# 64x32 in place of 64x64 tiles on TensorE for both layers of a convolution and GELU network

## The chip, the cores and the metric

The kernel runs on one core of a Trainium2 chip. The metric is device time in microseconds (us), the time of the one core. TensorE (PE in the profile) multiplies; a weight load (PEld) puts the stationary operand into its array and a matmul streams the moving operand through it. ScalarE is ACT, VectorE is DVE, GpSimd is POOL, and SP's queue issues most DMAs.

## What is computed

A causal depthwise convolution with 7 taps over 8 sequences of 4096 tokens and 192 channels, with softmax weights that each group of 24 channels shares, and behind it two dense layers with an exact GELU between them.

```python
def _attn_ref(x, weight):                      # x 8 x 4096 x 192, weight 8 x 7
    w = softmax(weight, axis=-1)
    x_pad = concatenate([zeros((B, 6, D)), x], axis=1)
    idx = arange(S)[:, None] + arange(7)[None, :]
    x_unf = x_pad[:, idx, :].reshape(B, S, 7, 8, 24)
    return einsum('hk,bskhg->bshg', w, x_unf).reshape(B, S, D)

def _moe_ref(x, w_in, w_out):                  # 32768 x 192, 192 x 2048, 2048 x 192
    h = x @ w_in
    g = 0.5 * h * (1.0 + erf(h / sqrt(2)))
    return g @ w_out
```

## The kernel before

**Blocks.** The 32768 tokens are cut into two halves of 16384 that are worked on together: the lower 64 partitions hold one half, the upper 64 the other, each with 64 of the 192 channels, in three passes (NP = 3). The tokens of a half come in blocks: six of 256 (n = 0 to 5), then 29 of 512 (n = 6 to 34; M0 is 6, M1 is 34).

**One block.** SP loads the tokens, VectorE transposes them (L516) and runs the convolution tap by tap (L537, L544), the last tap writing `xc` in bf16. In the first two blocks TensorE does the convolution instead (`pconv`, L708), with diagonal weights. Then the first layer: `mm1(n, i)` (L729) makes one slice of `hp`, 128 of the 2048 hidden units by 512 tokens of both halves. ScalarE applies GELU from `hp` to `gT` (L674), one slice at a time; `hp` has two buffers. The second layer multiplies `gT` by `wout` into `ob`.

**Tiles of TensorE.** A matmul names a tile of the 128x128 array by `tile_position=(row, column)`. The moving operand's 64 partitions choose the row half (0 or 64), the output's partitions choose the column strip. Matmuls on different tiles can run side by side.

First layer, L766: for each slice three passes p, in each both row halves `hf`, and within these `fw` output rows at a time (`fo`). In the 256-token blocks and block 6, `fw` is 128 (one 64x128 tile for each row half; 64 in two slices of block 0); in blocks 7 to 34, `M0 < n <= M1`, it is 64: four 64x64 tiles in the order (0,0), (0,64), (64,0), (64,64), twelve matmuls a slice, each over 512 tokens. Each row half has its own PSUM bank (offset `o`).

Second layer, L837, in `mm2_t(m, ps, i)` (L821) for blocks 6 to 33: three passes `ps`, in each 16 steps `i`, and in a step two row halves `hf` by two token halves `h`: four 64x64 tiles in the same order, each over 512 tokens. Here `wout` is stationary, `gT` moves, and the output is 64 channels by 512 tokens in a bank of `ob`; `h` chooses output partitions 0 to 63 or 64 to 127. VectorE transposes the finished bank into `osb` (L343), and SP stores it. Blocks 0 to 5 use an older form (`mm2`, L806), and the last block a 128x128 form (L889).

**Order on TensorE.** It is written out by hand. While block n's first layer runs, the second layer of block n - 1 is dealt out between its slices: after slice i come `SHARE[i]` of its 48 units, `(ps, i)`. Waits on semaphores stand at the head of a slice (GELU has emptied the buffer two slices back, L735; the convolution is done, L740 and L757) and at the head of a pass of the second layer (L826, L828, L831). The last matmul of a slice adds to `S_MM1`, which lets GELU start; the last one of a pass adds to `S_PH` or `S_MM2`, which lets VectorE empty the bank.

Of the kernel before, what the change touches and what calls it, by code (L numbers as in the profile page):

```python
# [11 lines left out]
def bass_lightweight_conv__then__act_gelu_exact_kernel(  # L12
# [10 lines left out]
    F2, C = moe_w_out.shape  # L23
# [18 lines left out]
    NP = D // 64  # L42
    NF = F // 128
# [29 lines left out]
    M0, M1 = 6, NB - 1  # L73
# [13 lines left out]
    CH = [[2 * CG[hf][i // 2] + i % 2 for i in range(NF)] for hf in range(2)]  # L87
# [9 lines left out]
    def sbt(name, shape, dt):  # L97
        return es.enter_context(nc.sbuf_tensor(name, shape, dt))
# [7 lines left out]
    def ap(t, off, pat):  # L106
        return bass.AP(t, off, pat)

    with es:
        win = sbt("win", [128, NP * F], BF16)  # L110
        wout = sbt("wout", [128, NF * C], BF16)
# [16 lines left out]
        gT = [sbt("gT%d" % i, [128, NF * 2 * TB], BF16) for i in range(2)]  # L128
# [38 lines left out]
        def bank(b, r=slice(0, 128), w=512):  # L167
            return ob[r, 512 * (b % 4) : 512 * (b % 4) + w]
# [4 lines left out]
        def hbuf(u, r=slice(0, 128), o=0, w=2 * TB):  # L173

            if u < SL0[1] and u % 3 == 2:
                return ob[r, 2 * TB + o : 2 * TB + o + w]
            return hp[u % 3 if u < SL0[1] else u % 2][r, o : o + w]
# [36 lines left out]
        def wait_pc(e, n, p):  # L214

            if n == 0:
                e.wait_ge(S_PCA, p + 1)
                if p >= 1:
                    e.wait_ge(S_PCE, p)
            else:  # L220
                e.wait_ge(S_PCA, len(PA) + 1)
                if p >= 1:
                    e.wait_ge(S_PCE, len(PV) + (0, 2, 5)[p])
# [31 lines left out]
        def cvd(n):  # L255

            return sum(NCV - 2 * (m in K0) for m in range(n + 1) if m not in PC)
# [6 lines left out]
        def banks(m, g):  # L264


            if m < M0:
                return [bank(2 * ((G0[m] + g) % 2) + h, w=C) for h in range(2)]
            if g % 2:
                return [hp[g // 2][:, h * TB : h * TB + C] for h in range(2)]  # L270
            r = NP * (M1 - 1 - M0)
            return [bank(b, w=C) for b in sorted((b % 4 for b in ((r + 3, r), (r + 1, r + 2))[g // 2]))]
# [60 lines left out]
        def ring(m, j):  # L333
            return NP * (m - M0) + j
# [350 lines left out]
        def _(t):  # L685
# [43 lines left out]
            def mm1(n, i):  # L729
                w, c = WS[n], NCH[n]  # L730
                u = SL0[n] + i
                if n == 0 and u >= 3:
                    t.wait_ge(S_GELU, u - 2)
                elif u >= SL0[1]:
                    t.wait_ge(S_GELU, u - 1)  # L735
                if i == 0:
                    if n in PC:
                        wait_pc(t, n, NP - 2)
                    else:
                        t.wait_ge(S_CV, cvd(n) - 1)  # L740
                if n == 0:
                    for j in {0: (0, 1), 2: (2, 5), 4: (3,), 6: (4,)}.get(i, ()):
                        t.wait_ge(S_WIN[j], 16)
                    if i in (1, 3, 4, 6):
                        t.wait_ge(S_DUPE, (0, 1, 0, 3, 4, 0, 5)[i])
                        if i == 1:
                            t.wait_ge(S_DUPP, 1)
                todo = [(cc, p) for cc in range(c) for p in range(NP)]
                head = (n, i) == (0, 0)
                if head:  # L750
                    todo.sort(key=lambda q: q[1] == NP - 1)
                for cc, p in todo:
                    if i == 0 and cc == 0 and p == NP - 1:
                        if n in PC:
                            wait_pc(t, n, p)
                        else:
                            t.wait_ge(S_CV, cvd(n))  # L757
                    for hf in range(2):
                        r = slice(64 * hf, 64 * hf + 64)
                        ch = CH[hf][i * c + cc]  # L760
                        f0 = FQ * ((ch // 2) ^ hf) + ch % 2
                        fw = 64 if (n == 0 and 4 <= i <= 5) or M0 < n <= M1 else 128
                        for fo in range(0, 128, fw):
                            f1 = 64 * hf * NP * F + p * F + f0 + 2 * fo
                            o = hf * TB + cc * w
                            ins = t.matmul(  # L766
                                hbuf(u, slice(fo, fo + fw), o, w),
                                ap(win, f1, [[NP * F, 64], [2, fw]]),
                                xc[n % 2][r, p * TB : p * TB + w],
                                start=(p == 0 and (cc == 0 or not head)),  # L770
                                stop=(p == NP - 1 and (cc == c - 1 or not head)),
                                tile_position=(64 * hf, fo),
                            )
                ins.then_inc(S_MM1)
# [46 lines left out]
            def mm2_t(m, ps, i):  # L821

                w = WS[m]
                if i == 0:
                    if ps < 2:
                        t.wait_ge(S_EV, EVC[m] - (1 if m == M0 else 2) + ps)  # L826
                    if ps > 0:
                        t.wait_ge(S_PH, PHC[m] + ps)  # L828
                if ps == 0 and i % 4 == 0:

                    t.wait_ge(S_GELU, SL0[m] + i + 4)  # L831
                for hf in range(2):
                    j = UPLO[ps][hf]
                    r = slice(64 * hf, 64 * hf + 64)
                    for h in range(2):
                        c0 = (2 * i + h) * w
                        ins = t.matmul(  # L837
                            bank(ring(m, j), slice(64 * h, 64 * h + 64), w),
                            ap(
                                wout,  # L840
                                64 * hf * NF * C + CH[h][i] * C + j,
                                [[NF * C, 64], [NP, 64]],
                            ),
                            gT[m % 2][r, c0 : c0 + w],
                            start=(i == 0 and (ps == 0 or (ps, hf) == (1, 1))),
                            stop=(i == NF - 1 and (ps == 2 or (ps, hf) == (1, 0))),
                            tile_position=(64 * hf, 64 * h),
                        )
                if i == NF - 1:
                    ins.then_inc(S_MM2 if ps == 2 else S_PH)  # L850

# [12 lines left out]
            for n in range(NB):  # L864
                todo = units(max(n - 1, 0))
                if n < 2:
                    todo = [(g, ph, k) for ph, k0, k1 in ORD0 for g in range(2) for k in range(k0, k1)]
                    todo = todo[12:] if n else todo[:12]
                for i in range(NSL[n]):
                    mm1(n, i)  # L870
                    for q in behind.get((n, i), []):
                        pconv(*q)
                    new = M0 < n <= M1
                    ws = SHARE if new else [0] * 7 + [1] if n == 0 else [1] * NSL[n]
                    a0 = len(todo) * sum(ws[:i]) // sum(ws)
                    a1 = len(todo) * sum(ws[: i + 1]) // sum(ws)
                    for un in todo[a0:a1]:
                        if n < 2 and un[:2] == (0, int(un[2] // 4 == 1)) and un[2] % 4 == 0:
                            t.wait_ge(S_WOUT[un[2] // 4], 16)
                        (mm2_t if new else mm2)(max(n - 1, 0), *un)  # L880
            m = NB - 1
            for g in range(NG[m]):
                wait_banks(t, m, g)
                for h in range(2):
                    for i in range(NF):
                        if (g, h) == (0, 0) and i % 4 == 0:
                            t.wait_ge(S_GELU, SL0[m] + i + 4)
                        c0 = (2 * i * NG[m] + 2 * g + h) * 128
                        ins = t.matmul(  # L889
                            banks(m, g)[h],  # L890
                            gT[m % 2][:, c0 : c0 + 128],
                            wout[:, CH[h][i] * C : (CH[h][i] + 1) * C],
                            start=(i == 0),
                            stop=(i == NF - 1),
                        )
# [47 lines left out]
```

## Time and profile before

| what | value |
|---|---|
| two runs, median | 678.76 us (678.42 and 679.11) |
| the profiled execution's span | 676.8 us |
| granted TensorE clock in the span | 1.000 |
| matmuls and weight loads | 12504 of each |
| L766 on 64x64 tiles, 512 tokens | 5376 matmuls, 376 ns each; 64x64 loads 107 ns |
| L837 on 64x64 tiles, 512 tokens | 5376 matmuls, 376 ns each; 64x64 loads 118 ns |
| first and last start of these matmuls | 83.37 and 663.35 us |
| GELU of one slice (L674) | 1023 ns |

The span reaches from the program's first to its last instruction in one profiled execution; the runs' time also holds what lies around it. In a row of the groups the columns are the line, the engine, the operation, output and inputs with their shapes, and the count; behind the bar the busy time and the mean time of one, and behind the next bar the engine's idle time before them and what ended it. Ends of matmuls are modelled, so that several matmuls overlap in the trace: the distance of their starts tells the pace, not their length.

### The profile page before, as it was taken

To read this page: it belongs to the slowest core of one execution; us is meant where nothing else is said; L and a number is where in the kernel's file an instruction comes from. 1 tells how busy PE (TensorE), PEld (TensorE's weight loads), DVE (VectorE), ACT (ScalarE), POOL (GpSimd) and SP (SyncE) were. 2 spreads that over 40 slices of the span, in tenths; PEclk is the share of its full clock that TensorE was granted. 3 is DMA by queue.
4 is the path that set the end of the run, shared out by engine and by line. 5 is a ranking of instruction groups with operands and counts; after the bars stand their busy time and mean duration, and the time that the engine had idled before them with its cause. 6 is when DMAs were issued, how large, how long until landed. Compare 5 with 4: busy or idle time off the path is not lost.

```text
span 676.8 us, 26873 instructions
## 1 busy us (share of the span) xinstructions
PE 673.1 (99%) x12504; PEld 413.7 (61%) x12504; DVE 526.4 (78%) x607; ACT 536.5 (79%) x551; POOL 35.7 (5%) x61
## 2 busy tenths in 40 slices
PE   9999999999999999999999999999999999999998
PEld 8999555555555555555555555555555555555557
DVE  6989977987778977779777788777797777887511
ACT  8998977887778777777877787877877777778773
POOL 7010000000000000000000000000000000000000
PEclk9999999999999999999999999999999999999999
DMA  9435324223444224442234431244422344310223
GB/s 155 117 93 122 72 60 96 71 46 76 96 95 92 50 52 96 95 96 67 43 84 96 95 91 44 57 96 95 96 58 51 84 96 95 83 42 22 49 48 95
DMA packets 133280, 53.64 MB, mean 79 GB/s; under 512 B 126384, under 2 KB 133104, under 8 KB 133168
## 3 DMA queue, kind: packets, MB, share of 16 engines
q1 hardware_dynamic: 129136, 49.37, 32.6%
q0 software_dynamic: 2912, 1.97, 2.0%
q8 instruction: 98, 1.61, 1.0%
q10 hardware_dynamic: 1120, 0.59, 0.3%
q14 instruction: 14, 0.11, 0.1%
HBM read 28.31 MB, written 25.17 MB: 79 GB/s over the span
## 4 chain that ended last, share of the span: by engine, by line
PE 98%; ACT 1%; DVE 0%; DMA 0%; issue 0%; ACTq 0%
PE hp L766 49%; PE ob L837 43%; PE ob L806 5%; PE ob L889 1%; PE hp L889 1%; ACT gT L674 1%; DMA wsb<-in_weight_dram 0%; ACT xc L210 0%; PE ob L708 0%; ACT dg L621 0%; DVE wcol L488 0%; ACT osb L314 0%; ACT wex L608 0%; ACT xTb L238 0%; DVE wnm L479 0%
## 5 line engine op out<-in xcount | busy, mean ns | idle before, releaser
L674 ACT ACTIVATE gT<-hp 128x1024 bf16<-128x1024 f32 x510 | 520.9, 1023 | 127.6 <-PE hp L766 123.9
L766 PE MATMUL hp<-xc,win 64*64 64x512 bf16 (+2 forms) x6036 | 417.3, 366 | 0.3
L837 PE MATMUL ob<-gT,wout 64*64 64x512 bf16 x5376 | 366.4, 376 | 0.0
L544 DVE SCALAR_TENSOR_TENSOR acc<-xT,wcol,acc 128x1024 f32<-128x1024 f32 (+1 forms) x330 | 295.4, 945 | 3.5 <-ACT acc L645 3.5
L766 PEld LDWEIGHTS hp<-xc,win 64*64 64x64 bf16 (+1 forms) x6036 | 189.3, 106 | 131.4 <-issue 0.3
L837 PEld LDWEIGHTS ob<-gT,wout 64*64 64x64 bf16 x5376 | 172.3, 118 | 122.8
L343 DVE STREAM_TRANSPOSE osb<-ob 128x512 f32<-128x512 f32 x84 | 74.4, 888 | 129.1 <-PE ob L837 129.1
L516 DVE STREAM_TRANSPOSE xT<-xin 128x1536 f32<-128x1536 f32 (+2 forms) x39 | 74.8, 1925 | 2.0 <-DMA xin<-in_x_dram 2.0
L544 DVE SCALAR_TENSOR_TENSOR xc<-xT,wcol,acc 128x1024 bf16<-128x1024 f32 (+1 forms) x66 | 60.6, 958 | 0.0
L443 POOL COPY xT<-xT 128x18 f32<-128x18 f32 x30 | 22.6, 753 | 510.3 <-DVE xT L516 487.0
L806 PE MATMUL ob<-wout,gT 64*128 64x192 bf16 x768 | 41.6, 243 | 0.0
L806 PEld LDWEIGHTS ob<-wout,gT 64*128 64x128 bf16 x768 | 34.2, 94 | 4.2
L537 DVE TENSOR_SCALAR acc<-xT,wcol 128x512 f32<-128x512 f32 (+2 forms) x60 | 33.7, 604 | 1.1
L688 PE MATMUL hp<-const-bfloat16-1.0 128*128 128x128 bf16 x48 | 4.8, 295 | 0.8 <-PEq L928 0.8
L889 PE MATMUL ob<-wout,gT 128*128 128x192 bf16 x64 | 5.6, 246 | 0.0
L889 PE MATMUL hp<-wout,gT 128*128 128x192 bf16 x64 | 5.6, 246 | 0.0
L889 PEld LDWEIGHTS ob<-wout,gT 128*128 128x128 bf16 x64 | 5.2, 98 | 0.4 <-issue 0.4
L889 PEld LDWEIGHTS hp<-wout,gT 128*128 128x128 bf16 x64 | 5.3, 98 | 0.0
L645 ACT ACTIVATE acc<-xT,wcol 128x256 f32<-128x256 f32 (+1 forms) x9 | 5.2, 575 | 0.0
L688 PEld LDWEIGHTS hp<-const-bfloat16-1.0 128*128 128x128 bf16 x48 | 4.7, 140 | 0.8 <-issue 0.8
L299 ACT ACTIVATE osb<-ob 128x384 f32<-128x384 f32 x10 | 4.9, 488 | 0.0
L314 ACT ACTIVATE osb<-hp 128x192 f32<-128x192 f32 x2 | 0.7, 330 | 4.6 <-PE hp L889 4.6
(42 smaller groups left out, 42.5 us busy)
## 6 DMA issues: line engine op xcount, KB each, us to landing
out_dram<-osb SPq DMA_DIRECT2D x124, 192.0 KB, 3.1
xin<-in_x_dram SPq DMA_DIRECT2D x116, 192.0 KB, 4.0
xin<-in_x_dram SPq DMA_DIRECT2D x18, 96.0 KB, 2.5
wout<-in_moe_w_out_dram POOLq DMA_DIRECT2D x4, 192.0 KB, 5.4
win<-in_moe_w_in_dram POOLq DMA_DIRECT2D x4, 96.0 KB, 4.0
win<-in_moe_w_in_dram POOLq DMA_DIRECT2D x2, 192.0 KB, 4.9
xin<-in_x_dram POOLq DMA_DIRECT2D x4, 96.0 KB, 4.2
out_dram<-osb ACTq DMA_DIRECT2D x4, 96.0 KB, 2.3
```

The lines of the kernel that those rows point to most:

```text
L343: v.transpose(ap(osb[m % 2], j, [[8 * C, 128], [C // 2, TB // 32], [NP, 32]]), bank(ring(m, j)),).then_inc(S_EV)
L443: g.tensor_copy(dst, src).then_inc(S_HALO)
L516: v.transpose(out, src).then_inc(S_TR)
L537: ins = v.tensor_scalar(a, src, wk, None, ALU.mult)
L544: ins = v.scalar_tensor_tensor(dst, src, wk, a, op0=ALU.mult, op1=ALU.add)
L645: a.activation(out=acc[n % 2][:, p * TB : p * TB + w], in_=ap(xT[n % 2], p * XW + HX, [[NP * XW, 128], [1, w]]), func=AF.Copy, scale=wcol[ ...
L674: a.activation(out=ap(gT[n % 2], i * c * 2 * w, dst), in_=ap(ob, 2 * TB, [[4 * TB, 128], *src[1:]]) if u < SL0[1] and u % 3 == 2 else ap(h ...
L688: t.matmul(hp[1][:, 0:128], one, one)
L766: ins = t.matmul(hbuf(u, slice(fo, fo + fw), o, w), ap(win, f1, [[NP * F, 64], [2, fw]]), xc[n % 2][r, p * TB : p * TB + w], start=(p == 0 ...
L806: ins = t.matmul(bb[sub], gT[m % 2][r, c0 : c0 + 128], wout[r, CH[sub][i] * C : (CH[sub][i] + 1) * C], start=(ph == 0 and k == 0), stop=(p ...
L837: ins = t.matmul(bank(ring(m, j), slice(64 * h, 64 * h + 64), w), ap(wout, 64 * hf * NF * C + CH[h][i] * C + j, [[NF * C, 64], [NP, 64]],) ...
L889: ins = t.matmul(banks(m, g)[h], gT[m % 2][:, c0 : c0 + 128], wout[:, CH[h][i] * C : (CH[h][i] + 1) * C], start=(i == 0), stop=(i == NF - 1),)
```

## The change

Two edits. In the first layer, `fw` is 32 for blocks 7 to 34, so that each 64x64 tile of a slice is two 64x32 tiles beside each other, and a pass has eight matmuls in the order (0,0), (0,32), (0,64), (0,96), (64,0), ... In the second layer each matmul of `mm2_t` is cut in the same way by a loop over `co`: 32 of its 64 output channels each, the same moving operand, the same bank, 32 partitions further. Waits, semaphore updates, operands, the order of steps, buffers and DMAs stay. The stationary operand of one matmul has 32 columns in place of 64, and matmuls and weight loads of these blocks double in number.

```diff
@@ mm1
-                        fw = 64 if (n == 0 and 4 <= i <= 5) or M0 < n <= M1 else 128
+                        fw = 32 if M0 < n <= M1 else 64 if n == 0 and 4 <= i <= 5 else 128
                         for fo in range(0, 128, fw):
@@ mm2_t
                     for h in range(2):
                         c0 = (2 * i + h) * w
-                        ins = t.matmul(
-                            bank(ring(m, j), slice(64 * h, 64 * h + 64), w),
-                            ap(
-                                wout,
-                                64 * hf * NF * C + CH[h][i] * C + j,
-                                [[NF * C, 64], [NP, 64]],
-                            ),
-                            gT[m % 2][r, c0 : c0 + w],
...
-                            tile_position=(64 * hf, 64 * h),
-                        )
+                        for co in range(0, 64, 32):
+                            ins = t.matmul(
+                                bank(ring(m, j), slice(64 * h + co, 64 * h + co + 32), w),
+                                ap(
+                                    wout,
+                                    64 * hf * NF * C + CH[h][i] * C + j + NP * co,
+                                    [[NF * C, 64], [NP, 32]],
+                                ),
+                                gT[m % 2][r, c0 : c0 + w],
...
+                                tile_position=(64 * hf, 64 * h + co),
+                            )
```

## Prediction

> **What bounds the kernel now.** I read the page first: engines, chain, groups.
>
> ```profile
> span 676.8 us, 26873 instructions
> PE 673.1 (99%) x12504; PEld 413.7 (61%) x12504; DVE 526.4 (78%) x607; ACT 536.5 (79%) x551; POOL 35.7 (5%) x61
> ...
> PE 98%; ACT 1%; DVE 0%; DMA 0%; issue 0%; ACTq 0%
> ...
> L674 ACT ACTIVATE gT<-hp 128x1024 bf16<-128x1024 f32 x510 | 520.9, 1023 | 127.6 <-PE hp L766 123.9
> ...
> L837 PE MATMUL ob<-gT,wout 64*64 64x512 bf16 x5376 | 366.4, 376 | 0.0
> ```
>
> TensorE is the bound: 98% of the chain that ended last, and no idle time before L837. ScalarE's GELU (L674) waits for TensorE, not the other way round. DMA has no share of the chain. So only TensorE's pace matters, as long as its neighbours keep up.
>
> "Busy" says nothing of that pace, since matmuls overlap; the timeline does. Its columns are first start, time from first start to last end, engine, line, shape and count. First a piece from the middle of the 512-token blocks, then a piece from the start of the kernel, where narrower and wider tiles run with fewer columns:
>
> ```profile
> 299.66 0.39 PE L837 MATMUL ob<-gT,wout 64*64 64x512 bf16 x4
> 299.88 0.82 PE L766 MATMUL hp<-xc,win 64*64 64x512 bf16 x12
> 300.52 0.82 PE L837 MATMUL ob<-gT,wout 64*64 64x512 bf16 x12
> ```
>
> ```profile
> 9.68 0.84 PE L766 MATMUL hp<-xc,win 64*128 64x256 bf16 x12
> ...
> 11.42 0.92 PE L766 MATMUL hp<-xc,win 64*64 64x256 bf16 x24
> 12.08 0.92 PE L766 MATMUL ob<-xc,win 64*64 64x256 bf16 x24
> 12.75 0.64 PE L708 MATMUL ob<-xTb,dg 64*64 64x128 bf16 x28
> ```
>
> In the first piece four 64x64 matmuls last 0.39 us from first start to last end, though one alone lasts 0.376: the four run side by side, their starts about 0.01 us apart in all. Three such groups go by from 299.88 to 300.52, so a group takes 0.213 to 0.216 us. The windows of L766 and L837 give it exactly: from 83.37 to 663.35 us each line ran 5376 matmuls, 10752 in 579.98 us, which is 2688 groups of four at **215.8 ns**. This stretch is the part that the change touches. The rest is 676.8 - 580.0 = 96.8 us and stays.
>
> **The change, part by part.**
>
> What it removes and adds: in blocks 7 to 34 of the first layer (L766) and 6 to 33 of the second (L837) each 64x64 matmul becomes two 64x32 matmuls over the same 512 columns. Products per line go from 5376 to 10752, and weight loads with them. A group is now eight tiles (two row halves by four strips of 32 output rows); both lines go through the eight in the same order, so a tile's next turn always comes eight matmuls later. The number of groups stays 21504 / 8 = 2688. Nothing is moved past a queue: no wait, no semaphore update and no DMA is added or removed; the update still sits on the last matmul of its step.
>
> Step 1, the pace of a group. Each tile must still stream 512 columns. What could change is the fixed part that a group pays beside the streaming. Two tiles of 64x128 with 256 columns: 12 matmuls from 9.68, last start at 9.68 + 0.84 - 0.27 = 10.25, so six groups of two with five periods in about 0.55 us, 0.11 each. Four tiles of 64x64 with 256 columns: 24 matmuls from 11.42 to 12.08, six groups of four in 0.66 us, 0.110 each. Two tiles and four tiles have the same period to about 1 ns. From 256 to 512 columns it grows by 215.8 - 110 = 105.8 ns, so 256 columns cost 105.8 and the fixed part is 110 - 105.8 = 4.2 ns (rounding included), whatever the number of tiles. No row shows eight tiles. Going by the step from two to four I take +0 ns a group, and bounds of 1 ns either way: 2688 x 1 = 2.7 us. From below the outer bound is the whole fixed part, 4.2 ns x 2688 = 11.3 us.
>
> Step 2, issue. Eight pairs of weight load and matmul must go out in 215.8 ns: 27.0 ns a pair, 13.5 ns an instruction. Now it is 54 and 27. The rows above show the new rate: 48 pairs from 11.42 to 12.75 are 27.7 ns a pair, and that is set by their 256 columns. The 28 pairs of L708 (128 columns) have their last start at 12.75 + 0.64 - 0.22 = 13.17, so 0.42 us for 27 gaps, 15.6 ns a pair, 7.8 ns an instruction. They could not stand ready beforehand as a whole, if the wait ahead of them holds the sequencer: the casts that they wait for (L210, L212) end at 12.63 in the timeline and the first load starts at 12.72. So 13.5 ns an instruction is covered by a factor of 1.7 over 56 instructions, but not shown over thousands; over those the trace has only 27 ns. Cost taken: 0. If the cover is gone, see rival A.
>
> The Trainium skill has a rule against this step. "Runtime: NRT & Kernel Launch", section "Instruction fetch mechanics", speaks of a floor of about 20 cycles for each instruction at the sequencer, and "Advanced Engine Details and Errata", section "Clock Domains", gives that sequencer 1.2 GHz: an estimate of 16.7 ns, 267 ns for sixteen instructions, 137 us over 2688 groups, about 816 us in all. I go by the rows: 7.8 ns an instruction over 28 pairs is under half of that rule.
>
> Step 3, weight loads. The groups with shapes give 107 ns (L766) and 118 ns (L837) for a 64x64 load, under a stream of 215.8 ns on the same tile: the cover is the tile's own previous matmul. With half the columns and twice the count, each load still has a whole period of its tile. The L708 row shows four loads every 4 x 15.6 = 62 ns; eight at that rate need 125 of the 215.8. Cost taken: 0.
>
> Step 4, instruction fetch. The queue table has 98 instruction pages of 16 KB in the span, 256 instructions each, at 1.0% of 16 engines: 0.010 x 16 x 676.8 / 98 = 1.1 us a page, one every 6.9 us. 21504 further instructions are 84 pages more, one every 3.5 us. 1.1 fits into 3.5. Cost 0.
>
> Step 5, neighbours. The last tile of a group starts some 15 ns later than now, so a GELU may start that much later; it has about 0.3 us of idle time before it (123.9 us over 409 waits), which covers it. The moving operand is now read for four strips in place of two. In the window of one block (144.13 to 164.85 us) ScalarE and VectorE are busy 16.37 and 16.76 us of 20.72, so they would have to slow by 24% before TensorE waited. From one strip (66 to 82 us) to two (300 to 340 us) GELU stayed at 1023 ns and L544 went from 1279 to 1271. Cost 0.
>
> Sum on the profiled execution: 676.8 + 0 = 676.8 us. The median of the runs, 678.76, lies 1.96 above that span, so **679 us**. With 1 ns a group either way: 676 to 682.
>
> **The rivals.** 2% is 13.6 us, about what a measurement of this kernel can tell from no change; it is 13.6 / 2688 = 5.05 ns a group. That is the point from which every rival below decides.
>
> A (slower): weight loads or issue come to light, sixteen instructions a group not going out within 215.8 ns. Place: before the first tile of each group in L766 and L837. For it: the new rate is shown for 48 pairs at most. Against it: those rows, and the loads' cover. Price: the nearest row is the first load of L708, 12.72, and its matmul, 12.75: 30 ns from an uncovered load to its matmul at 64 columns, so 15 ns at half the columns, 40 us in all, **719 us**. At the other end a whole load of 118 ns a group is 317 us, 996 us.
>
> B (slower): the eight tiles do not all run side by side, for instance because four strips can't all be fed at once. For it: no row of the trace has more than two strips. Against it: from one strip to two nothing was lost. Price at the full: four at a time, two rounds a group, +580 us, **1259 us**; at 10% of the streaming 58 us, 737 us.
>
> C (the change does nothing of note, but a little faster): the fixed part vanishes: 678.8 - 11.3 = **667 us**, 1.7%. For it: only that the fixed part has no named cause. Against it: it was alike for two tiles and four. Even at its full price it stays within 2%. Faster by more than 2% would need streaming itself to be quicker, and the windows of L766 and L837 already show a granted clock of 1.00.
>
> **How the numbers follow.** Forecast (no change) 0.72; C 0.02; A 0.16; B 0.08; 0.02 for faster by over 2%, by something that no row shows. Within 2%: 0.72 + 0.02 = 0.74. Slower by over 2%: 0.16 + 0.08 = 0.24. Range: the likeliest case alone holds 676 to 682; its 0.72 is short of 8 in 10, so I go up to A's lower price, 719, which takes in about half of A (0.08). Left out are the other half of A, B, C and gains over 2%: 0.08 + 0.08 + 0.02 + 0.02 = 0.20. Range 676 to 719.
>
> **What the changed profile would show.** Step 1 right: the windows of L766 and L837 hold 10752 matmuls each in 580 us, and the timeline has eight starts within some 25 ns, then a gap, one group every 216 ns. Step 2 or 3 wrong: idle time or "issue" before PE matmuls, starts spread evenly over the group instead of bunched, a period of over 221 ns. If the period is about 267 ns the floor of an instruction was real. Step 4 wrong: single long gaps about every 128 pairs instead of a longer period everywhere. Step 5 wrong: GELU over 1023 ns, and TensorE waiting for ACT at L766. B: a period near 430 ns, or a stretch of streaming in all groups with no waiting anywhere. What would make the prediction wrong is above all that eight tiles are outside every row that I extrapolate from.

## The result and the profile after

The changed kernel takes 750.38 us (747.94 and 752.81) against 678.76: a ratio of 1.1045, 95% interval 1.095 to 1.114. It is 71.6 us slower, outside the predicted 676 to 719.

The page of the changed kernel. L838 is the second layer's line now:

```profile
span 751.1 us, 48377 instructions
PE 699.0 (93%) x23256; PEld 420.2 (56%) x23256; DVE 534.1 (71%) x607; ACT 536.5 (71%) x551; POOL 36.1 (5%) x61
...
q8 instruction: 182, 2.98, 1.7%
...
PE 92%; issue 6%; DMA 1%; POOL 0%; DVE 0%; ACT 0%; POOLq 0%
...
L674 ACT ACTIVATE gT<-hp 128x1024 bf16<-128x1024 f32 x510 | 520.8, 1024 | 201.3 <-PE hp L766 198.2
L766 PE MATMUL hp<-xc,win 64*32 64x512 bf16 (+1 forms) x11412 | 508.2, 372 | 21.5 <-issue 20.1
L838 PE MATMUL ob<-gT,wout 64*32 64x512 bf16 x10752 | 461.6, 378 | 26.8 <-issue 24.8
```

The new thing is "issue": 6% of the chain, and idle time before both lines that nothing in the profile ends. TensorE waits for no engine and no data. GELU still takes 1024 ns and only waits longer for TensorE.

Where in time? The window of L766 from the first to the last start of the 64x32 matmuls (length, busy time of PE and PEld with counts, clock, DMA share, GB/s):

```profile
83.98:737.70 653.72, 457.48 (x10752) 198.05 (x10752) 1.00 0.30 67
```

653.72 us in place of 579.98 for 2688 groups: 73.7 of the 74.3 us that the profiled span grew by lie here. But they aren't spread over the groups. The timeline of TensorE, from 94 to 104 us:

```profile
93.91 1.01 PE L766 MATMUL hp<-xc,win 64*32 64x512 bf16 x24
94.56 0.40 PE L838 MATMUL ob<-gT,wout 64*32 64x512 bf16 x7
95.17 0.83 PE L838 MATMUL ob<-gT,wout 64*32 64x512 bf16 x17 [0.21 <-issue]
95.62 1.02 PE L766 MATMUL hp<-xc,win 64*32 64x512 bf16 x24
96.27 1.02 PE L838 MATMUL ob<-gT,wout 64*32 64x512 bf16 x24
96.92 1.02 PE L766 MATMUL hp<-xc,win 64*32 64x512 bf16 x24
97.56 1.24 PE L838 MATMUL ob<-gT,wout 64*32 64x512 bf16 x32
98.43 1.29 PE L766 MATMUL hp<-xc,win 64*32 64x512 bf16 x24
...
101.93 1.30 PE L838 MATMUL ob<-gT,wout 64*32 64x512 bf16 x24
```

Undisturbed, 24 matmuls have 0.65 us from one row to the next, as 12 had before: three groups of eight at 0.216. So eight tiles run side by side at the full pace, and of 2725 distances between groups 2432 are 215 to 219 ns. In between are holes: after 7 matmuls at 94.56 the eighth comes at 95.17; the rows of 98.43 and 101.93 last 1.29 and 1.30 us instead of 1.02.

The holes have an address. I numbered TensorE's instructions in the order of their starts. In a count by 256 the 64x32 stretch has 168 borders, and at 112 of them there is a hole (over 260 ns between two starts), always at place 193 or 194 of the count. Together these holes are some 67 us longer than the normal distance, of 74 that the profiled span grew by. The trace has 46631 instructions of TensorE and 182 packets of 16 KB on q8, the instruction queue: 256 instructions a packet, which I call a page. In the trace each hole ends 1.2 to 1.7 us (median 1.4) after the end of such a packet. The DMA view of the same 94 to 104 us, in 40 slices of 0.25 us:

```profile
GB/s 0 0 0 0 0 0 0 0 66 0 0 0 0 0 0 0 0 0 0 0 0 0 0 66 0 0 0 0 0 0 0 0 0 0 0 0 0 0 66 0
...
q8 instruction: 3, 0.05, 2.2%
```

Nothing but three instruction pages moves, one after the border at 95.17 (in the slice from 96.00), one after that near 98.9 (from 99.75), one after that near 102.6 (from 103.50). So a page seems to be asked for only when the border before it is crossed. The 112 holes agree: behind each of them the packet for the next page starts 1.03 to 2.79 us after the hole's end, never before it. For the first two: 1.03 and 1.10 us from the border to the packet, 1.23 and 1.39 for the packet, 1.47 and 1.24 until the first instruction of the new page. Each sum is 3.73 us, and TensorE now uses a page up in 16 groups of 216 ns, 3.45 us.

The longest hole cost twice. In the windows (length, busy time of PE, PEld, DVE, ACT, POOL, clock, DMA share, GB/s):

```profile
281.90:284.20 2.30, 0.00 (x0) 0.00 (x0) 0.00 (x0) 0.00 (x0) 0.00 (x0) 1.00 1.02 180
284.30:287.60 3.30, 3.30 (x72) 1.67 (x80) 0.00 (x0) 1.46 (x2) 0.00 (x0) 0.54 0.05 12
```

For 2.3 us and more nothing runs while data moves at 180 GB/s; then the clock is granted at about half for 3.4 us, and groups take 427 ns. The Trainium skill, "TensorE: Matmul & The Clock Gate", section "Why this matters for your kernels", warns of idle gaps over some 3 us; here a distance of 2.76 us between two starts was followed by the half clock, and the next longest, 2.35 us, was not. That is about 2 us of the 74.

### The profile page after: what moved, and what is told of

It reads as the page before. It is cut to its first block, busy times and chain, and to the rows that moved or that the text cites. A ratio compares the mean times of both kernels' runs of the same rounds, so it can differ in the third digit from the quotient of the medians.

```text
span 751.1 us, 48377 instructions
## 1 busy us (share of the span) xinstructions
PE 699.0 (93%) x23256; PEld 420.2 (56%) x23256; DVE 534.1 (71%) x607; ACT 536.5 (71%) x551; POOL 36.1 (5%) x61
## 4 chain that ended last, share of the span: by engine, by line
PE 92%; issue 6%; DMA 1%; POOL 0%; DVE 0%; ACT 0%; POOLq 0%
PE hp L766 45%; PE ob L838 41%; PE ob L806 4%; PE ob L890 1%; PE hp L890 1%; DMA win<-in_moe_w_in_dram 1%; POOL win L393 0%; PE ob L708 0%; POOL xTb L240 0%; DVE win L247 0%; PE ob L766 0%; DVE xT L516 0%; POOL idb L400 0%; ACT osb L314 0%; DVE idb L468 0%
## 5 line engine op out<-in xcount | busy, mean ns | idle before, releaser
L674 ACT ACTIVATE gT<-hp 128x1024 bf16<-128x1024 f32 x510 | 520.8, 1024 | 201.3 <-PE hp L766 198.2
L766 PE MATMUL hp<-xc,win 64*32 64x512 bf16 (+1 forms) x11412 | 508.2, 372 | 21.5 <-issue 20.1
L838 PE MATMUL ob<-gT,wout 64*32 64x512 bf16 x10752 | 461.6, 378 | 26.8 <-issue 24.8
L766 PEld LDWEIGHTS hp<-xc,win 64*32 64x32 bf16 (+1 forms) x11412 | 228.5, 93 | 162.9 <-issue 47.4
L838 PEld LDWEIGHTS ob<-gT,wout 64*32 64x32 bf16 x10752 | 207.3, 97 | 158.0 <-issue 57.8
L343 DVE STREAM_TRANSPOSE osb<-ob 128x512 f32<-128x512 f32 x84 | 78.1, 932 | 195.0 <-PE ob L838 194.8
L516 DVE STREAM_TRANSPOSE xT<-xin 128x1536 f32<-128x1536 f32 (+2 forms) x39 | 79.8, 2054 | 3.1 <-DMA xin<-in_x_dram 3.0
L708 PE MATMUL ob<-xTb,dg 64*64 64x256 bf16 (+1 forms) x112 | 3.6, 245 | 0.5 <-ACT xTb L238 0.3
```

What stands on the lines that cost most here:

```text
L343: v.transpose(ap(osb[m % 2], j, [[8 * C, 128], [C // 2, TB // 32], [NP, 32]]), bank(ring(m, j)),).then_inc(S_EV)
L516: v.transpose(out, src).then_inc(S_TR)
L674: a.activation(out=ap(gT[n % 2], i * c * 2 * w, dst), in_=ap(ob, 2 * TB, [[4 * TB, 128], *src[1:]]) if u < SL0[1] and u % 3 == 2 else ap(h ...
L766: ins = t.matmul(hbuf(u, slice(fo, fo + fw), o, w), ap(win, f1, [[NP * F, 64], [2, fw]]), xc[n % 2][r, p * TB : p * TB + w], start=(p == 0 ...
L838: ins = t.matmul(bank(ring(m, j), slice(64 * h + co, 64 * h + co + 32), w), ap(wout, 64 * hf * NF * C + CH[h][i] * C + j + NP * co, [[NF * ...
```

## The experiments

Theory F: TensorE runs out of instructions at page borders; what counts is instructions per time, not the shape of the tiles. Theory T: an eight-tile group costs 27 ns more in itself. "Before" is 678.6 to 678.9 us in these runs.

**One layer alone.**

```diff
 e1: fw = 32 if M0 < n <= M1 ...       (first layer; mm2_t as before)
 e2: mm2_t with co, 64x32              (second layer; fw as before)
```

> Only the first layer is on 64x32 tiles; the second layer stays on 64x64. Theory F (TensorE runs out of instructions at the borders of 256-instruction pages): eight-tile and four-tile groups mix to 12 instructions in 215.8 ns, a page lasts 256 / 12 x 215.8 ns = 4.6 us, longer than most of the pages took to arrive in the changed kernel (median 3.9 us from one stalled border to the next, 90% under 4.9), so nearly all of the loss goes: 680 to 690 us. Theory T (an eight-tile group itself costs 27 ns more, whatever supplies it): half of the loss, about 714 us.

> Only the second layer is on 64x32 tiles; the first stays on 64x64. The same sums as for the first layer alone. Theory F: 680 to 690 us. Theory T: about 714 us.

Measured: 797.13 us (1.174, 1.1712 to 1.1767) and 793.46 us (1.1687, 1.1664 to 1.171). Both theories missed: half of the change costs more than the whole. The timeline of e1:

```profile
299.49 0.40 PE L766 MATMUL hp<-xc,win 64*32 64x512 bf16 x8
299.82 0.86 PE L837 MATMUL ob<-gT,wout 64*64 64x512 bf16 x12
300.61 0.84 PE L766 MATMUL hp<-xc,win 64*32 64x512 bf16 x24
```

From the last 64x32 group (299.49) to the first 64x64 group is 0.33 us in place of 0.216, and the three 64x64 groups and the change back take 0.79 in place of 0.65. Over the trace: 330 ns at a change to 64x64, 316 at a change to 64x32, and the second group after a change is up to 40 ns late. There are 32 changes of size in each of 28 blocks, 896: 118.6 / 896 = 0.132 us each, and 114.9 / 896 = 0.128 us in e2. The weight loads show where:

```profile
299.82 0.39 PEld L837 LDWEIGHTS ob<-gT,wout 64*64 64x64 bf16 x12 [0.42 <-issue]
300.60 0.35 PEld L766 LDWEIGHTS hp<-xc,win 64*32 64x32 bf16 x24 [0.40 <-issue]
```

The first load of the other size starts only with its own matmul's group (299.82, 300.60), whereas loads of the same size start a group ahead (in the kernel before at 300.31 for matmuls at 300.52). What the two changes cost at the group itself, 114 and 100 ns, is near the length of one load of the new size (120 and 91 ns by the groups of e1), as if one load lay open at each change; that this is the cause is not shown. For F and T the time of these runs says nothing, but their traces do: eight-tile groups follow each other at 216 ns (227 to 234 right behind a change), with no hole at a page border. That speaks against T.

**The instructions without the tiles.**

```diff
 mm1, blocks 7 to 34, and mm2_t: 64x64 tiles as before
+for kc in range(2):              # outside hf
+    # moving operand and output: columns 256 * kc to 256 * kc + 256
+    # start only at kc == 0, stop only at kc == 1
```

> The tiles stay 64x64, four side by side, but each matmul of 512 tokens is cut into two of 256, with a weight load each: as many instructions as in the changed kernel, on the tile shape of the kernel before. Two groups of 256 columns take 2 x 109.2 ns in place of 215.8, +7 us over 2688. Theory F: the loss of the changed kernel comes back, 679 + 7 + 72 = 758 us (745 to 770), with stalls every 256 instructions. Theory T: 686 us.

Measured: 757.2 us (1.1155, 1.1115 to 1.1195). The prediction of F was 758, of T 686. In its page, with four 64x64 tiles, the same signs stand:

```profile
span 755.0 us, 48377 instructions
...
q8 instruction: 182, 2.98, 1.7%
...
PE 92%; issue 6%; DMA 1%; POOL 0%; DVE 0%; ACT 0%; POOLq 0%
```

Here 117 of 168 borders have a hole, and every hole between groups in the stretch is at a border. T falls: the shape of the tiles isn't needed for the loss.

**The data out of the way.**

```diff
 load:  nb = 1 if n >= 9 else mb                          # blocks of 32 tokens
 store: 1 if m >= 9 else WS[m] // 32                      # likewise
```

> The changed kernel, but from block 9 on every load and every store moves a sixteenth of its bytes (one run of 96 numbers a row block in place of 16), so that the tokens and most of the output of these blocks are left out; DMAs and semaphores stay in number. Theory F with data transfers in the way of the instruction pages: the shortest parts seen (1.03 us from the border to the packet, 0.88 for the packet, 1.22 to the next instruction) make 3.1 us, under the 3.45 that a page lasts, so the stalls go from block 9 on: about 690 us. Theory F with a page's delay as it is, whatever else moves: 740 to 750 us. Theory T: 750 us.

Measured: 730.82 us (1.0767, 1.071 to 1.0824), between the two forms of F. The bytes went from 73 to 24 GB/s and the long holes with them, but not the short ones:

```profile
span 728.7 us, 48377 instructions
...
q1 hardware_dynamic: 31216, 11.76, 7.0%
...
PE 96%; issue 4%; ACT 0%
```

Where two borders in a row have a hole, the median distance is 3.76 us (3.86 in the changed kernel), and the 90% mark 4.02 (4.85). What fell is above all the time from a border to the next packet: median 1.23 us (1.38), 90% mark 1.68 (2.14). So of some 72 us, 20 came from pages that queued behind data, and 52 from the page's own way, 3.7 us. My sum of the shortest parts, 3.1 us, was too short: they do not fall together.

**How many instructions are too many.** 64x64 tiles with the columns cut in two for a part of the work, so without any change of tile size:

```diff
 e5:  first layer only
 e6:  first layer, and mm2_t where i % 3 == 0
 e9:  first layer, and mm2_t where i % 2 == 0
 e10: first layer, and mm2_t where i % 4 != 3
```

> 64x64 tiles throughout, the 512 columns cut into two matmuls of 256 in the first layer only: 12 instructions in 215.8 ns on average, as with one layer on 64x32 tiles, but with no change of tile size on the way. Theory F (a page of instructions arrives too late): a page lasts 4.6 us; summing what the stalls of the two kernels with 16 instructions exceed 1.15 us by leaves 4 to 5 us, and the shorter matmuls cost 3.5: 687 us (683 to 695). A cost for each added instruction (theory L): half of what the cut of both layers cost, 679 + 39 = 718 us.

> 64x64 tiles throughout, the 512 columns cut into two matmuls in the first layer and in six of the sixteen steps of each pass of the second: 13.5 instructions in 215.8 ns, a page lasts 4.1 us. Theory F: the stalls of the kernels with 16 instructions, each less 0.65 us, leave 12 to 14 us, the shorter matmuls cost 5: 697 us (688 to 708). Theory L: 0.69 of 79 us, 733 us.

> 64x64 tiles, the columns cut in two in the first layer and in eight of the sixteen steps of each pass of the second: 14 instructions in 215.8 ns on average, a page lasts 3.95 us. Theory F with a lead (TensorE's queue holds about 64 instructions, a quarter of a page, so that a page may be late by a quarter of its length at no cost, as long as the pages arrive in time on average): the typical page (3.76 to 3.9 us from border to border where both stall) is still in time, only those beyond 4.9 us, about one in ten, cost some tenths of a us: 6 us, and the shorter matmuls 5: 690 us (685 to 700). Theory L (a cost for each added instruction): 0.75 of 79 us, 738 us.

> As the run with 14 instructions, but twelve of the sixteen steps are cut: 15 instructions in 215.8 ns, a page lasts 3.68 us, now under the typical 3.76 to 3.9. Theory F: the lead is used up and each of some 155 pages costs about 0.25 us, 39 us, and the shorter matmuls 6: 724 us (705 to 735). Theory L: 0.875 of 79 us, 748 us.

| run | instructions in 216 ns | a page lasts, us | borders with a hole | measured, us | F said | L said | ratio, 95% |
|---|---|---|---|---|---|---|---|
| e5 | 12 | 4.6 | 0 of 126 | 681.66 | 687 | 718 | 1.003 to 1.006 |
| e6 | 13.5 | 4.1 | 4 of 142 | 685.54 | 697 | 733 | 1.0079 to 1.0117 |
| e9 | 14 | 3.95 | 19 of 147 | 692.2 | 690 | 738 | 1.0151 to 1.0206 |
| e10 | 15 | 3.68 | 49 of 157 | 726.26 | 724 | 748 | 1.0657 to 1.0724 |
| e3 | 16 | 3.45 | 117 of 168 | 757.2 | 758 | | 1.1115 to 1.1195 |

It is a knee, not a slope. A cost for each instruction is out: e5 adds half of e3's instructions and 3 us, which is what its shorter groups cost (2 x 109.2 ns in place of 215.8). Beside what the shorter groups cost, some 2 us are lost at 4.1 us a page, 8 at 3.95, 41 at 3.68 and 72 at 3.45. e5 and e6 came out 1 to 3 us below the ranges that F gave, which counted every late page. For the runs with 14 and 15 instructions F was given a lead as well (some 64 instructions ahead of TensorE cover a page that is late now and then), and these two fit within 3 us. In e10 that is luck in part: F spread the loss over all of some 155 pages at 0.25 us, and the trace has it in fewer and longer holes.

The lead can be read from the traces. At a hole the next packet starts 1.03 us or more after the page's first instruction. In the kernel before it starts up to 0.75 us ahead of it, and in e5 up to 0.27. The differences, 1.78 us at 27 ns an instruction and 1.30 us at 18, are 66 and 72 instructions: an estimate of how far the request runs ahead of the matmuls while nothing is late.

Waits of TensorE in e5 and in e10 (engine and line, what ended the wait, us in total, times, longest):

```profile
PE hp L688 <- PEq L932: 0.8, 1, 0.8
```

```profile
PE hp L770 <- issue: 13.4, 19, 1.7
PE ob L845 <- issue: 12.9, 20, 1.5
```

In e5 only the wait before the first matmul of the kernel is left; in e10 both lines wait for "issue" again.

**Half as many changes of tile size.**

```diff
-            SHARE = [3, 3, 3, 3, 4, 3, 3, 3, 3, 4, 3, 3, 3, 3, 2, 2]
+            SHARE = [0, 6, 0, 6, 0, 7, 0, 6, 0, 7, 0, 6, 0, 6, 0, 4]   # e7: in e1; e8: in the kernel before
```

> First layer alone on 64x32 tiles, as before, but the second layer's steps are dealt out after every second slice, in sixes: 448 changes of tile size in place of 896. Theory S (TensorE loses about 0.13 us at each change of tile size, 118 us over 896): half of that goes, 679 + 59 = 738 us. If the 118 us come from the mixed instruction rate or from one layer's tiles, 797 us as with short runs.

> The kernel before with the second layer's steps dealt out in sixes, nothing else changed: the control for the run above. Order alone should cost nothing: 679 us (677 to 682). If GELU no longer hides behind two slices in a row it shows here, as TensorE waiting for ACT.

Measured: e7 749.35 us (1.1037, 1.1021 to 1.1054), e8 691.59 us (1.0187, 1.017 to 1.0204). The control missed: the new order costs 12.9 us by itself, 9.4 of it with one distance of some 0.55 us in place of 0.216 between two groups of the second layer in each of 28 blocks. Its waits show where it is (0.2 us is the idle time behind the modelled end of the matmul):

```profile
PE ob L837 <- PE ob L837: 4.6, 28, 0.2
```

Taken against its control, e7 loses 57.8 us over 448 changes, 0.129 us each; e1 had 0.132. So a change between 64x64 and 64x32 costs 0.13 us here, and that is all that e1 and e2 lost.

## Why the prediction was wrong

**The bound** was read rightly: TensorE's pace sets the time in both kernels, and its neighbours keep up.

**Step 1 was right.** Eight tiles take a group in 216 ns, as four did. By single starts the groups of 256 columns were 109.2 ns apart and not 110, so the fixed part is 2.6 ns in place of 4.2; the forecast doesn't rest on it. Of what the prediction feared most, that eight tiles lie outside every row, nothing came true: rival B is out.

**Step 2 was right at its place.** Sixteen instructions go out in 216 ns, 13.5 ns each, for as long as a page lasts. The prediction's estimate from the Trainium skill ("Runtime: NRT & Kernel Launch", "Instruction fetch mechanics", with a floor of 20 cycles) would have had all groups at 267 ns; it came to 816 us, and the runs show no such floor. The same section says of crossing a 16 KiB border that its cost is mostly hidden. At 27 ns an instruction this case agrees (the kernel before has no such hole); at 13.5 it does not: 112 of 168 borders show. The 28 pairs that step 2 took as its cover are 56 instructions, fewer than the lead of some 66: that row could have been fed by instructions that stood ready, and says nothing of whether pages arrive in time.

**Step 3 was right.** No hole lies anywhere but at a page border or a half-clock stretch, and loads of 93 to 97 ns stay covered.

**Step 4 failed**: "one every 3.5 us. 1.1 fits into 3.5. Cost 0." It set the packet's own 1.1 us against the length of a page and put the rest of the page's way at nothing. What counts is the way from one border to the next, since the next page is not under way before: 1.0 to 1.4 us to the packet, some 1.1 for it, 1.4 after it, by the medians 3.7 to 3.9 us in all, against 3.45. That made the 67 us at 112 borders. The trace of before had rows to warn of this:

```profile
q8 instruction: 98, 1.61, 1.0%
...
wout<-in_moe_w_out_dram POOLq DMA_DIRECT2D x4, 192.0 KB, 5.4
...
out_dram<-osb SPq DMA_DIRECT2D x4, 96.0 KB, 2.2
```

Its DMA issues took 2.2 to 5.4 us from issue to landing. They move 6 or 12 times the bytes of a page, so they are a bound and no price; but in e4 issues of 12 KB, less than a page, still took 1.5 and 1.9 us. Had I bounded a page by these rows, step 4 would have been a rival with 3.45 us as its point of decision: at 3.7 us it gives (3.7 - 3.45) x 168 = 42 us, at 3.9 us 76 us. The sign of the failure stood in the prediction, "single long gaps about every 128 pairs instead of a longer period everywhere", but with no price.

**Step 5 was right** for the time: GELU 1023 to 1024 ns, and no matmul of the two layers waits for ScalarE or VectorE; three weight loads of L766 wait for GELU, 2.7 us in all.

**Rival A** had the right sign and a wrong place and mechanism. Its instructions do not go out too slowly; for a while there are none. e3 shows that the 64x32 tiles are not needed. It has as many weight loads as the changed kernel, so it doesn't clear the loads; what does is the place of the holes, at page borders and not before the first tile of each group.

What stays open: what the 1.0 to 1.4 us before a packet and the 1.4 us after it consist of, and why only one page is under way. No run here takes them apart.

## What to carry to other kernels

Cutting matmuls into smaller tiles gives no more work per time when the tiles are already full, but it takes instructions, and they have a supply of their own: somewhere between 15.4 ns an instruction (e9, 19 of 147 borders with a hole) and 14.4 ns (e10, 49 of 157), over more than a page of 256, TensorE here began to lose much time at page borders. Price a supply by the time from request to use, not by the transfer's own length, and ask whether the next request can be under way meanwhile. And changing the tile size between steps cost 0.13 us each time here, so that half a retiling can be dearer than a whole one.

## What was not expected of the hardware

With 64x32 tiles VectorE's transposes are longer, though nothing waits for them: L516 from 2316 to 2490 ns and L343 from 888 to 932, by the groups with shapes. With as many instructions on 64x64 tiles (e3) they are 2336 and 898, so the count alone doesn't do it; with little data traffic (e4) they stay at 2453 and 946. One layer alone on 64x32 hardly does it either: 2351 and 907 in e1, 2315 and 889 in e2, where the eight-tile groups come at a slower rate. GELU on ScalarE shows nothing of the kind. I tried nothing that would tell why.
